# Attention and a GELU network in one kernel: filler matmuls, batch 0's v behind its k, masks as items of their own, late query tiles in the next chunk's layer 1

## The chip, the core and the metric

The kernel runs on one core of a Trainium2 chip. Five engines work side by side, each through its own program in order: TensorE (PE: matrix products from the on-chip memory SBUF into PSUM), VectorE (DVE), ScalarE (ACT: exponential, GELU), GpSimd (POOL) and SyncE (SP). An engine that has to wait for another holds up all that stands behind in its own program. POOL and SP also issue the transfers (DMAs); those from POOL can change the type from 32-bit to 16-bit floats on the way. The metric is the device time of one execution in microseconds; lower is better.

## The reference

Two parts, one after the other. First causal attention over 8 batches and 8 heads, 576 positions of 64 elements, with a decay that a running sum over the positions makes:

```python
scores = scale * np.matmul(q, k.transpose(0, 1, 3, 2))
causal = np.triu(np.ones((S, S), dtype=bool), k=1)
cum = np.cumsum(np.maximum(s, 0.0), axis=-1)
bias = -(cum[:, :, :, None] - cum[:, :, None, :])
scores = np.where(causal, -1000000000.0, scores + np.minimum(bias, 0.0))
scores = scores - np.max(scores, axis=-1, keepdims=True)
attn = np.exp(scores)
attn = attn / (np.sum(attn, axis=-1, keepdims=True) + 1e-09)
attn_out = np.matmul(attn, v)
```

Then, with the eight heads side by side, x has 4608 rows (tokens) of 512, and goes through a network of two layers with 2048 units:

```python
h = x @ w_in
g = 0.5 * h * (1.0 + erf(h * inv_sqrt2))
out = g @ w_out
```

## The kernel before

Matrix products run on 16-bit inputs. The decay makes far keys vanish, so the kernel computes scores for a band of key and query blocks alone, and at its end tests from the data that this was allowed (`cert_1` to `cert_4`); a general path behind a branch is there for other data and isn't taken here.

**Tiling.** The 4608 tokens are cut into nine chunks of 512. A batch has 576 tokens, in five query tiles `it` of 128 (the last of 64). Heads go in two groups `g` of four, and the band's scores of a group come in two units `u`, each of 128 x 512 for each head. So a batch has four score items `sc(b, g, u)` and ten items `av(b, g, it)` that multiply by v. Tiles 0 and 1 need unit 0 alone, tile 2 both units, tiles 3 and 4 unit 1.

**The work of a batch b.** `load_qks(b)` has 16 transfers on POOL's queue (L91) and `load_v(b)` five (L113, SP's queue; POOL's for batch 1). `tr_qk` (L177, VectorE) transposes q and k, `den_col` (L208) and `scale_v` (L200, VectorE) put v with its weights into `vv`, `absmax` (L184, VectorE, 2.5 us each) and `square_v` (L192, ScalarE) gather what the test at the end needs. `sc_item` computes scores (L320, TensorE), their exponentials (L328, ScalarE) into P, and multiplies the blocks on the diagonal by a triangular mask (L332, and L337 for unit 1, VectorE). `av_item` multiplies (L396, TensorE), then VectorE takes the reciprocal of the sums (L405) and scales into `x` (L406). With the second group done, `to_xT` writes the transposed tile into `xT`: by DMA from SP's queue (L375) in batches above 0, by TensorE (L379) and a VectorE copy (L382) in batch 0. In batch 0 `sc_first` takes the place of `sc_item`: the mask is added on TensorE (L362).

**The network on a chunk c.** `l1_item(c, f2)` for f2 = 0 to 7: eight matmuls (L424) into PSUM `h_ps`, then a GELU on ScalarE (L429) into `gT`. It reads all 512 tokens of the chunk in `xT` at once (chunk 0: in halves of 256). `l2_item` then takes the four row blocks (`sub`) of 128 tokens, sixteen matmuls each (L440) into PSUM `o_ps`, a VectorE copy (L447) and a DMA to the output (L449).

**Order.** It is written out by hand. While chunk c is in layer 2, the attention of batch b = c + 1 is woven in: `groups` cuts a row block into four slots of four matmuls and runs side items after each. Preparation of batch b on VectorE (`tr_qk`, `den_col`, `scale_v`, `absmax`) stands between layer 1 and layer 2 of chunk c in the program (L529 to L536); VectorE reaches it early, since little of its program lies in layer 1. Chunk 8 has no attention beside it, and neither has layer 2 of chunk 7. Chunk c reaches into batch c by 512 - 64c tokens: query tiles 0 to 3 of batch 1 for chunk 1, tiles 0 to 2 for chunks 2 and 3, tiles 0 and 1 for chunks 4 and 5, tile 0 for 6 and 7.

**Buffers.** In PSUM, two of tag `sc` (scores and `h_ps`, two banks each), two of `av`, two of `mlp` (`o_ps` and the filler's output). In SBUF, two each of P, raw q/k, raw v, `qkT` and `vv`, six of `x`, one `gT`. So row block n + 2 waits for the copy of row block n, and an av item waits for the scaling of the av item two before.

**The head.** POOL issues q and k of batch 0, then eight weight blocks (`load_w`, L137), then q and k of batch 1, then v of batch 1. At most eight of its transfers are under way: each issue from the ninth on waits for the one eight before it.

The layer 2 of chunks 1 to 6 stands in the program so:

```python
groups(c, (0,), [[], [], [(sc, b, 0, 0)], []])
groups(c, (1,), [[(sc, b, 1, 0)], [], [(sc, b, 0, 1), (av, b, 0, 0)], [(av, b, 0, 1)]])
groups(c, (2,), [[(sc, b, 1, 1), (gelu_set,), (av, b, 1, 0)], [(av, b, 1, 1)], [(av, b, 0, 2)], [(av, b, 0, 3), (av, b, 0, 4)]])
groups(c, (3,), [[(av, b, 1, 2)], [(av, b, 1, 3)], [(av, b, 1, 4)], []])
```

## Time and profile before

| | us |
|---|---|
| median of 3 runs | 350.01 |
| lowest, highest | 348.54, 350.91 |
| the profiled execution, its own time | 350.83 |
| its span in the profile | 349.1 |

| stage | from, to | span |
|---|---|---|
| head | 0 to 31.0 | 31.0 |
| chunk 0, layer 1 | 31.0 to 49.9 | 18.9 |
| chunk 0, layer 2 | 49.9 to 77.2 | 27.3 |
| chunk 1 | 77.2 to 112.0 | 34.8 |
| chunk 2 | 112.0 to 148.3 | 36.3 |
| chunks 3 to 6 | 148.3 to 286.6 | 138.3 |
| chunk 7 | 286.6 to 314.9 | 28.3 |
| chunk 8 and the end | 314.9 to 349.1 | 34.2 |

How to read the lines below. The page gives busy time of each engine, and the chain of work that ended last, followed back from the end. A line of the timeline has start and duration in us, engine, line of the kernel, operation, output and inputs, shape and count; in brackets stands the engine's idle time before it and what ended it. A line of the chain has start, duration and what it was. A row of busy time by stage has the stretch, its length, busy time (and instructions) of PE, PE's weight loads, DVE, ACT and POOL, the clock granted to TensorE, the DMA share and GB/s. Matmuls are pipelined and their ends are modelled, so the time from one start to the next says more than a duration; some matmul records are missing, so a count of 63 can stand for 64.

### The profile page before, as it was taken

The page shows a single profiled execution, that of the slowest core. Times are in us where ns is not written, and L with a number is a line of the kernel's source. Part 1 is how long each engine was busy: PE and PEld are TensorE (multiplying, and loading weights), DVE is VectorE, ACT ScalarE, POOL GpSimd, SP SyncE. Part 2 cuts the span into 40 slices and gives each one's busy share as a digit, 9 for nine tenths or more (in the row PEclk, how much of TensorE's full clock was granted, in tenths as well). Part 3 has the DMA queues.
Part 4 walks back from the last instruction along what each step waited for, and adds up shares of the span by engine and source line. Part 5 has one row for each costly group of instructions (what it writes and reads, how often), then busy time and mean ns, then how long its engine had stood idle before and what let it go on. Part 6 is the DMA issues. An engine that isn't in the chain of part 4 may idle for free.

```text
span 349.1 us, 6207 instructions
## 1 busy us (share of the span) xinstructions
PE 316.1 (91%) x2467; PEld 156.4 (45%) x2508; DVE 187.7 (54%) x392; ACT 182.9 (52%) x243; POOL 88.0 (25%) x149
## 2 busy tenths in 40 slices
PE   0998997779999999799999999999999999999992
PEld 0326863444444444344444444444544444444441
DVE  7233688678458915891479247925792570141020
ACT  2433594728871887067727872777178715304400
POOL 8832598810460082008200640000000000000000
PEclk9999999989999999999999999999999999999998
DMA  8999999989594786478657685700410051020011
GB/s 98 210 206 207 148 190 116 178 154 223 85 140 115 173 82 100 108 173 82 85 107 188 64 105 107 188 2 32 120 39 0 33 121 39 0 90 33 1 61 68
DMA packets 98868, 37.27 MB, mean 107 GB/s; under 512 B 89776, under 2 KB 93872, under 8 KB 98832
## 3 DMA queue, kind: packets, MB, share of 16 engines
q0 software_dynamic: 43504, 14.82, 37.0%
q1 hardware_dynamic: 55328, 21.98, 25.0%
q8 instruction: 21, 0.34, 0.5%
q14 instruction: 15, 0.12, 0.1%
HBM read 36.85 MB, written 9.44 MB: 133 GB/s over the span
## 4 chain that ended last, share of the span: by engine, by line
PE 70%; DMA 12%; POOL 7%; ACT 4%; DVE 3%; issue 2%; POOLq 0%
PE h_ps L424 32%; PE o_ps L440 29%; DMA w_out_r<-in_moe_w_out_dram 6%; POOL raw_qk L91 6%; PE sc_ps L320 5%; PE av L396 4%; ACT P L328 4%; DMA raw_v<-in_v_dram 2%; DMA raw_qk<-in_k_dram 2%; DMA xT<-x 2%; DVE P L332 1%; DMA raw_qk<-in_q_dram 1%; DVE x L406 1%; POOL raw_v L113 1%; POOL w_out_r L137 1%
## 5 line engine op out<-in xcount | busy, mean ns | idle before, releaser
L440 PE MATMUL o_ps<-w_out_r,gT 128*128 128x512 bf16 x545 | 135.7, 382 | 3.7 <-DVE o_sb L447 2.0
L424 PE MATMUL h_ps<-xT,w_in_r 128*128 128x512 bf16 (+1 forms) x632 | 128.9, 361 | 4.9 <-DMA xT<-x 3.5
L429 ACT ACTIVATE gT<-h_ps 128x1024 bf16<-128x1024 f32 (+1 forms) x80 | 75.1, 938 | 103.2 <-PE h_ps L424 99.6
L424 PEld LDWEIGHTS <-w_in_r 128*128 128x128 bf16 x640 | 62.6, 99 | 67.9 <-issue 6.5
L440 PEld LDWEIGHTS <-gT 128*128 128x128 bf16 x576 | 51.2, 98 | 55.5 <-issue 6.1
L328 ACT ACTIVATE P<-sc_ps 128x1024 bf16<-128x1024 f32 x56 | 54.3, 1021 | 25.1 <-PE sc_ps L320 25.1
L91 POOL DMA_DIRECT2D raw_qk<-in_q_dram x64 | 38.8, 627 | 104.4 <-DVE amx L184 94.4
L332 DVE TENSOR_TENSOR P<-P,tri_bf 128x1024 bf16<-128x1024 bf16 x28 | 19.3, 691 | 68.7 <-ACT P L328 68.7
L447 DVE COPY o_sb<-o_ps 128x512 f32<-128x512 f32 x36 | 24.7, 686 | 49.5 <-PE o_ps L440 49.5
L91 POOL DMA_DIRECT2D raw_qk<-in_k_dram x64 | 38.7, 633 | 10.5 <-DMA w_out_r<-in_moe_w_out_dram 7.8
L184 DVE TENSOR_REDUCE amx<-raw_qk 128x2 f32<-128x2304 bf16 x16 | 40.0, 2536 | 0.0
L396 PE MATMUL av<-vv,P 128*128 128x65 bf16 x576 | 31.3, 200 | 8.6 <-DVE x L406 8.6
L396 PEld LDWEIGHTS <-P 128*128 128x128 bf16 x576 | 26.0, 102 | 26.4 <-DVE x L406 18.5
L406 DVE TENSOR_TENSOR x<-av,rc 128x256 bf16<-128x256 f32 (+1 forms) x80 | 33.8, 423 | 2.8
L200 DVE TENSOR_TENSOR vv<-raw_v,wb 128x512 bf16<-128x512 f32 (+1 forms) x40 | 25.6, 692 | 4.0 <-DMA raw_v<-in_v_dram 3.8
L177 DVE STREAM_TRANSPOSE qkT<-raw_qk 128x576 f32<-128x576 f32 x32 | 22.4, 749 | 6.4 <-DMA raw_qk<-in_q_dram 5.5
L192 ACT ACTIVATE sq<-raw_v 128x512 bf16<-128x512 f32 (+1 forms) x40 | 24.9, 623 | 0.0
L405 DVE RECIPROCAL rc<-av 128x4 f32<-128x4 f32 (+1 forms) x80 | 14.0, 175 | 20.0 <-PE av L396 19.9
L320 PE MATMUL sc_ps<-qkT 32*128 32x256 bf16 (+2 forms) x560 | 20.6, 250 | 0.0
L320 PEld LDWEIGHTS <-qkT 32*128 32x128 bf16 x560 | 13.0, 92 | 13.9 <-issue 13.0
L366 ACT ACTIVATE P<-sc_ps 128x1024 bf16<-128x1024 f32 x8 | 8.2, 1023 | 12.2 <-PE sc_ps L362 12.2
L354 PE MATMUL sc_ps<-qkT 32*128 32x256 bf16 (+2 forms) x80 | 10.4, 356 | 2.1 <-DVE qkT L177 1.4
(74 smaller groups left out, 82.8 us busy)
## 6 DMA issues: line engine op xcount, KB each, us to landing
out_dram<-o_sb SPq DMA_DIRECT2D x36, 256.0 KB, 2.2
raw_v<-in_v_dram SPq DMA_DIRECT2D x28, 256.0 KB, 3.9
raw_qk<-in_q_dram POOLq DMA_DIRECT2D x64, 72.0 KB, 2.9
raw_qk<-in_k_dram POOLq DMA_DIRECT2D x64, 72.0 KB, 3.1
w_in_r<-in_moe_w_in_dram POOLq DMA_DIRECT2D x4, 512.0 KB, 11.7
w_out_r<-in_moe_w_out_dram POOLq DMA_DIRECT2D x4, 512.0 KB, 18.2
raw_v<-in_v_dram POOLq DMA_DIRECT2D x4, 256.0 KB, 4.0
raw_v<-in_v_dram SPq DMA_DIRECT2D x7, 128.0 KB, 3.5
```

The source lines that it names most:

```text
L91: nc.gpsimd.dma_start(out=raws[b, "qk"][h * 32 : h * 32 + 32, i, g, :].rearrange("p (t c) -> p t c", c=2 * D), in_=bass.AP(tensor=src.tens ...
L184: nc.vector.tensor_reduce(amx[:, b * HG + g], raws[b, "qk"][:, :, g, :], axis=AX, op=ALU.max, apply_absolute_value=True,)
L192: nc.scalar.activation(sq[:n_st], raws[b, "v"][:n_st, st].rearrange("p h d -> p (h d)"), func=AF.Square, accum_out=sumv[:n_st, b, st : st ...
L200: nc.vector.tensor_tensor(vv[b % 2][:n_st, st, :, 0:D], raws[b, "v"][:n_st, st, :, :], w.unsqueeze(2).to_broadcast([n_st, H, D]), op=MULT,)
L320: nc.tensor.matmul(s_ps[h // 2][:, h % 2, off : off + n], lhsT=qk[r, 1, g, jt * 128 : jt * 128 + 128, e], rhs=qk[r, 0, g, i0 : i0 + n, e], ...
L328: nc.scalar.activation(P[:, 2 * h2 : 2 * h2 + 2, o : o + 512], s_ps[h2], func=AF.Exp, scale=scale)
L396: nc.tensor.matmul(o_ps[:, h, :], lhsT=P[:, h, off : off + 128], rhs=vv[b % 2][:, jt, 4 * g + h, :], start=(i == 0), stop=(i == len(BLK[it ...
L406: nc.vector.tensor_tensor(x_of[b, it][:n, g * 256 : g * 256 + 256].rearrange("p (h d) -> p h d", d=D), o_ps[:n, :, 0:D], rc[:n].unsqueeze( ...
L424: nc.tensor.matmul(h_ps[:, i, n0:n1], lhsT=w_in_r[:, ko, ft * 128 : (ft + 1) * 128], rhs=xT[:, ko, c * NB + n0 : c * NB + n1], start=(ko = ...
L429: nc.scalar.activation(gT_of[c][:, f2 * 2 : f2 * 2 + 2, n0:n1], h_ps[:, :, n0:n1], func=AF.Gelu)
L440: nc.tensor.matmul(y_of[c, sub], lhsT=gT[:, ft, sub * 128 : (sub + 1) * 128], rhs=w_out_r[:, ft, :], start=(ft == 0), stop=(ft == FT - 1),)
L447: nc.vector.tensor_copy(o_sb, y_of[c, sub])
```

## The change

- **Fillers.** `zero` is set first on VectorE, and dummy matmuls on zeros (`filler(n)`, 512 columns each) go into TensorE's program: 16 ahead of `weights()`, 4 behind it, and 6, 4, 4, 1 and 1 between the items of batch 0. The two memsets for `ident` and `uptri` pass from POOL to VectorE.
- **v behind k.** Of batch 0's v, tiles 0 and 1 stay on SP's queue; tiles 2 to 4 go to POOL's, behind batch 0's k and ahead of the weights. Scores of batch 0 fill both banks together, and their order with the v products is new. `masks()` stands later in the program.
- **Chunk 0, layer 2.** `absmax(1)` goes from ahead of layer 2 to behind it. Scores, masks and av items have new slots, `load_v(2)` is issued behind row block 1, query tile 4 of batch 1 goes to layer 1 of chunk 1, and tiles 2 and 3 are transposed by TensorE.
- **Masks apart.** `sc_item` ends with the exponentials; `mk_item` holds the multiplication by the mask, in a slot of its own.
- **Chunks 1 to 6, layer 2.** Score items stand in slots 2, 5, 7, 10 (batches 2 and 3) or 2, 5, 8, 11 of sixteen, masks in 5, 8, 11, 13 (14), av items of tiles 0 and 1 in 6, 7, 9, 10; in batches 2 and 3 tile 2 follows in 12 and 13.
- **Late query tiles.** The other av items of batch c (tile 4 for chunk 1, tiles 3 and 4 for chunks 2 and 3, tiles 2 to 4 from chunk 4 on) are woven into layer 1 of chunk c, one behind each step f2, and with them the preparation of batch c + 1.

```diff
+    zero = const.tile([128, NB], bf16, name="zero")
+    nc.vector.memset(zero, 0.0)
     ident = const.tile([128, 128], fp32, name="ident")
-    make_identity(nc, ident)
+    nc.vector.memset(ident, 0.0)
+    make_identity(nc, ident, nomemset=True)
...
+    def mk_item(b, g, u):
+        P = P_of[b, g]
+        o = UO[u]
         d = P[:, :, o : o + 512].rearrange("p e (g c) -> p e g c", c=256)[:, :, :, 0:128]
         nc.vector.tensor_tensor(
             d, d, tri_bf.unsqueeze(1).unsqueeze(1).to_broadcast([128, 4, 2, 128]), op=MULT
...
     exp_set()
+    filler(16)
     weights()
+    filler(4)
     tr_qk(0, 0, 0)
     v0 = raw_v(0)
-    nc.vector.memset(v0[0:1, :, 0, 0:1], 0.0)
-    load_v(0, nc.sync)
-    masks()
-    tr_qk(0, 1, 0)
+    nc.vector.memset(v0[0:1, 0:2, 0, 0:1], 0.0)
+    load_v(0, nc.sync, range(2))
+    load_v(0, nc.gpsimd, range(2, ST))
     for i in range(4):
         load_w(0, i)
     for i in range(4):
         load_w(1, i)
     load_qks(1)
     load_v(1, nc.gpsimd)
+    masks()
+    tr_qk(0, 1, 0)
     sc_first(0, 0)
+    filler(6)
     sc_first(0, 1)
+    filler(4)
     den_col(0)
     tr_qk(0, 0, 1)
     scale_v(0, 0)
+    tr_qk(0, 1, 1)
     scale_v(0, 1)
-    tr_qk(0, 1, 1)
+    sc_first(1, 0)
     av_item(0, 0, 0)
     av_item(0, 0, 1)
...
+    late_of = {1: [(0, 4), (1, 4)]}
+    for c in range(2, B):
+        late_of[c] = [(g, it) for it in range(3 if c < 4 else 2, ST) for g in range(HG)]
...
             for f2 in range(FT // 2):
                 l1_item(c, f2)
+                for g, it in late_of.get(c, [])[f2 : f2 + 1]:
+                    av(c, g, it)
+                if b < B and f2 < HG:
+                    tr_qk(b, 0, f2)
+                    tr_qk(b, 1, f2)
+                if b < B and f2 == 2:
+                    den_col(b)
+                    for st in range(2):
+                        scale_v(b, st)
+                if b < B and f2 == 3:
+                    for st in range(2, ST):
+                        scale_v(b, st)
+                if b < B and 4 <= f2 < 4 + HG:
+                    absmax(b, f2 - 4)
...
         if b < B:
-            for g in range(HG):
-                for i in range(2):
-                    tr_qk(b, i, g)
-            den_col(b)
-            for st in range(ST):
-                scale_v(b, st)
-            for g in range(HG):
-                absmax(b, g)
+            if c == 0:
+                for g in range(HG):
+                    for i in range(2):
+                        tr_qk(b, i, g)
+                den_col(b)
+                for st in range(ST):
+                    scale_v(b, st)
             exp_set()
             if c == 0:
                 l2_item(c, (0,))
-                groups(c, (1,), [[(sc, b, 0, 0)], [], [(sc, b, 0, 1)], []])
+                groups(c, (1,), [[], [(sc, b, 0, 0)], [], [(sc, b, 0, 1), (mk, b, 0, 0)]])
+                load_v(2, nc.sync)
+                groups(c, (2,), [
+                    [(av, b, 0, 0)],
+                    [(sc, b, 1, 0), (av, b, 0, 1)],
+                    [(mk, b, 0, 1)],
+                    [(sc, b, 1, 1), (av, b, 0, 2), (mk, b, 1, 0)],
+                ])
                 groups(c, (3,), [
+                    [(av, b, 1, 0)],
+                    [(av, b, 1, 1), (mk, b, 1, 1)],
+                    [(av, b, 0, 3), (av, b, 1, 2, True)],
+                    [(av, b, 1, 3, True), (to_xT, b, 2, True), (to_xT, b, 3, True)],
                 ])
...
+                side = [[] for _ in range(16)]
+                sc_at = (2, 5, 7, 10) if b < 4 else (2, 5, 8, 11)
+                for at, (g, u) in zip(sc_at, [(0, 0), (1, 0), (0, 1), (1, 1)]):
+                    side[at].append((sc, b, g, u))
+                side[sc_at[3]].append((gelu_set,))
+                for at, (g, u) in zip((5, 8, 11, 13 if b < 4 else 14), [(0, 0), (1, 0), (0, 1), (1, 1)]):
+                    side[at].append((mk, b, g, u))
+                for at, (g, it) in zip((6, 7, 9, 10), [(0, 0), (0, 1), (1, 0), (1, 1)]):
+                    side[at].append((av, b, g, it))
+                if b < 4:
+                    side[12].append((av, b, 0, 2))
+                    side[13].append((av, b, 1, 2))
+                for sub in range(4):
+                    groups(c, (sub,), side[4 * sub : 4 * sub + 4])
```

More of the change, by code (lines that the diff above doesn't have):

```diff
@@ L15 @@
 from concourse._compat import with_exitstack
-from concourse.masks import make_identity, make_upper_triangular
+from concourse.masks import make_identity
 @with_exitstack
@@ L161 @@
         nc.vector.memset(t[64:128, ST - 1, :, :], 0.0)
-    zero = const.tile([128, NB], bf16, name="zero")
-    nc.vector.memset(zero, 0.0)
     nc.vector.memset(sumv, 0.0)
@@ L308, with scores @@
     P_of, x_of = {}, {}
-    def sc_item(b, g, u):
-        if u == 0:
-            P_of[b, g] = work.tile([128, 4, PW], bf16, tag="P", bufs=2, name="P")
-        P = P_of[b, g]
-        qk = qkT[b % 2]
+    def scores(qk, g, u, masked=False):
         s_ps = [ps.tile([128, 2, 512], fp32, tag="sc", bufs=2, name="sc_ps") for _ in range(2)]
@@ L323, in sc_item @@
                         rhs=qk[r, 0, g, i0 : i0 + n, e],
-                        start=(e == 0), stop=(e == 1), tile_position=(h * 32, 0),
+                        start=(e == 0), stop=(not masked and e == 1), tile_position=(h * 32, 0),
                     )
+            for h in range(4 if masked else 0):
+                m = min(n, 128)
+                nc.tensor.matmul(
+                    s_ps[h // 2][:, h % 2, off : off + m], lhsT=ident_bf, rhs=neg_bf[:, :m],
+                    start=False, stop=True,
+                )
+        return s_ps
+    def sc_item(b, g, u):
+        if u == 0:
+            P_of[b, g] = work.tile([128, 4, PW], bf16, tag="P", bufs=2, name="P")
+        P = P_of[b, g]
+        s_ps = scores(qkT[b % 2], g, u)
         o = UO[u]
@@ L411, in av_item @@
         )
-        if g == HG - 1 and b > 0:
+        if g == HG - 1 and b > 0 and not later:
             to_xT(b, it)
```

83 lines of the change are left out of this document (29 added, 54 removed).

## The prediction

> **What bounds the kernel now.** I read the page first (busy shares, the chain that ended last), then busy time by stage, then the timeline where a stage holds idle TensorE.
>
> ```profile
> PE 316.1 (91%) x2467; PEld 156.4 (45%) x2508; DVE 187.7 (54%) x392; ACT 182.9 (52%) x243; POOL 88.0 (25%) x149
> PE 70%; DMA 12%; POOL 7%; ACT 4%; DVE 3%; issue 2%; POOLq 0%
> ```
>
> TensorE is 91% busy and 70% of the chain. Nothing here takes real TensorE work away, so a gain can only be idle or slow TensorE time. The stages, cut where layer 1 of a chunk starts (span, TensorE busy, VectorE busy in columns 2, 3 and 5):
>
> ```profile
> 49.90:77.20 27.30, 21.10 (x214) 10.85 (x216) 19.17 (x43) 14.72 (x23) 18.32 (x31) 0.94 1.17 151
> 77.20:112.00 34.80, 33.38 (x275) 15.94 (x281) 22.62 (x50) 21.55 (x28) 9.52 (x16) 1.00 0.80 145
> 112.00:148.30 36.30, 33.38 (x275) 15.90 (x280) 23.40 (x45) 21.55 (x28) 9.57 (x16) 1.00 0.69 116
> 148.30:286.60 138.30, 132.83 (x1100) 64.02 (x1121) 86.03 (x166) 86.19 (x112) 19.15 (x32) 1.00 0.48 90
> 286.60:314.90 28.30, 28.14 (x131) 12.68 (x132) 5.56 (x27) 8.18 (x8) 0.00 (x0) 1.00 0.16 45
> ```
>
> The first row is layer 2 of chunk 0, with 6.2 us idle. Then come chunk 1 (34.8), chunk 2 (36.3), chunks 3 to 6 (138.3, or 34.57 each) and chunk 7 (28.3), whose layer 2 has no attention beside it.
>
> **The head (fillers, v behind k).** Layer 1 of chunk 0, and the last key transpose ahead of it:
>
> ```profile
> 17.26 0.78 DVE L177 STREAM_TRANSPOSE qkT<-raw_qk 128x576 f32<-128x576 f32 x1 [0.58 <-DMA raw_qk<-in_k_dram]
> ...
> 31.00 1.87 PE L424 MATMUL h_ps<-xT,w_in_r 128*128 128x256 bf16 x8 [0.73 <-DVE xT L382]
> ...
> 35.27 1.11 PE L424 MATMUL h_ps<-xT,w_in_r 128*128 128x256 bf16 x8
> ```
>
> The same eight matmuls take 1.87 us at 31.0 and 1.11 at 35.3, so TensorE ran at half rate until about 35 us, whatever the clock column says. Fillers keep it busy from about 1 us, and should have it at full rate when the first scores come. After the key transpose (18.0) there remain two score items, four exponentials of 1.0 us (1.94 for two, below), the attention-times-v items and two transposes, some 7 us: layer 1 starts near 25 in place of 31. It lasts 18.9 us now (31.0 to 49.9) and loses about 2 us to the half rate, so layer 2 of chunk 0 starts near 42: a lead of 0 (no warming) to 9, I take 8. It is worth less than that, because of the next wait.
>
> **Layer 2 of chunk 0.** POOL's queue, the chain, and VectorE with TensorE:
>
> ```profile
> 36.90 0.60 POOL L91 DMA_DIRECT2D raw_qk<-in_k_dram  x1 [1.94 <-DMA w_out_r<-in_moe_w_out_dram]
> 39.45 0.60 POOL L91 DMA_DIRECT2D raw_qk<-in_k_dram  x1 [1.95 <-DMA w_out_r<-in_moe_w_out_dram]
> ...
> 44.78 4.26 POOL L113 DMA_DIRECT2D raw_v<-in_v_dram  x5
> ```
> ```profile
> 47.45 6.26 DMA raw_v<-in_v_dram
> ```
> ```profile
> 53.73 1.29 DVE L200 TENSOR_TENSOR vv<-raw_v,wb 128x512 bf16<-128x512 f32 x2 [2.41 <-DMA raw_v<-in_v_dram]
> ...
> 54.94 5.00 DVE L184 TENSOR_REDUCE amx<-raw_qk 128x2 f32<-128x2304 bf16 x2
> ...
> 59.86 0.67 DVE L447 COPY o_sb<-o_ps 128x512 f32<-128x512 f32 x1
> ...
> 60.59 1.02 PE L440 MATMUL o_ps<-w_out_r,gT 128*128 128x512 bf16 x4 [1.98 <-DVE o_sb L447]
> ```
>
> POOL issues one q/k load of batch 1 each time a weight block lands (every 2.55 us), the rest after the last one at 39.2, then v: batch 1's v lands at 53.7. The program still puts scale_v of batch 1 ahead of the copy of row block 0 on VectorE, and row block 2 needs that copy's PSUM buffer. Only the 5.0 us of absmax leave this place. So the copy comes at 55.0 and row block 2 can start at 55.7, not 60.59: 4.9 us won. With the full lead TensorE has done row blocks 0 and 1 by 50 and idles 5.9 us; with none it gets there at 58.6, and 2.0 are won. A lead above 3 us buys nothing.
>
> The three v loads of batch 0 that pass from SP's queue to POOL's, ahead of the weights, cost 0.9 us of issue each (4.26 for five). POOL's queue holds transfers then, so the weights land at the same rate and the bytes are the same; I bound their landing at 0.4 earlier (two memsets leave POOL) to 0.9 later (less v beside the q/k issue), and take 0, the nearest to the steady 2.55. POOL serves nothing else that waits.
>
> The gap has its own price:
>
> ```profile
> 69.86 1.90 PE L440 MATMUL o_ps<-w_out_r,gT 128*128 128x512 bf16 x4
> ...
> 77.24 2.97 PE L424 MATMUL h_ps<-xT,w_in_r 128*128 128x512 bf16 x13 [1.92 <-DMA xT<-x]
> ```
>
> Four matmuls took 1.90 us at 69.86, 1.02 at 60.59. After 2 us of idle (58.6 to 60.59) the rate held; after sparse work it was half. Dense work from 31.0 took 4.2 us to win it back, so I charge half of that, 2.1 us (0 to 4). The Trainium skill ("TensorE: Matmul & The Clock Gate", Part 1 and "HAM oscillation") speaks against the change here: an idle window of about 3.4 us halves the clock, and a busy one restores it. By that page the price would be half of 3.4 to 6.8, 1.7 to 3.4 us, and the sum 0.5 lower to 1.2 higher; the 69.86 row agrees that the rate falls, no row shows a clean 5.9 us gap.
>
> From row block 2 to layer 1 of chunk 1 it takes 16.65 us now (60.59 to 77.24). New: 32 matmuls at 0.216 (6.9), two score items (1.4), 56 av matmuls at 0.03 (1.7), half rate (2.1), waits for masks moved behind (0.9 + 0.8, worked out under chunks 1 and 2), and the last chain of av, reciprocal, scaling, TensorE transpose and two copies in place of the DMA transpose (2.4): 16.2. Layer 1 of chunk 1 starts at 71.9, not 77.24: **5.3 us won** (bounds 3 to 7.5). Absmax, cert_decay and 5 us of VectorE now lie in layer 1 of chunk 1, under 14 us of TensorE.
>
> **Chunks 3 to 6.** The layer 2 from 231.31 to 252.06, TensorE, then VectorE, then ScalarE:
>
> ```profile
> 231.31 2.75 PE L440 MATMUL o_ps<-w_out_r,gT 128*128 128x512 bf16 x11
> ...
> 236.39 0.89 PE L320 MATMUL sc_ps<-qkT 32*128 32x256 bf16 x16
> ...
> 243.34 0.30 PE L396 MATMUL av<-vv,P 128*128 128x65 bf16 x4 [0.73 <-DVE x L406]
> ...
> 246.12 0.41 PE L396 MATMUL av<-vv,P 128*128 128x65 bf16 x8 [0.36 <-DVE x L406]
> ...
> 249.85 0.41 PE L396 MATMUL av<-vv,P 128*128 128x65 bf16 x8
> 250.10 1.02 PE L440 MATMUL o_ps<-w_out_r,gT 128*128 128x512 bf16 x4
> ...
> 252.06 2.11 PE L424 MATMUL h_ps<-xT,w_in_r 128*128 128x512 bf16 x9
> ```
> ```profile
> 241.84 0.69 DVE L332 TENSOR_TENSOR P<-P,tri_bf 128x1024 bf16<-128x1024 bf16 x1 [1.95 <-ACT P L328]
> ...
> 242.65 0.17 DVE L405 RECIPROCAL rc<-av 128x4 f32<-128x4 f32 x1
> ...
> 250.29 0.18 DVE L405 RECIPROCAL rc<-av 128x4 f32<-128x4 f32 x1 [0.47 <-PE av L396]
> 250.51 0.42 DVE L406 TENSOR_TENSOR x<-av,rc 128x256 bf16<-128x256 f32 x1
> ...
> 252.26 0.69 DVE L447 COPY o_sb<-o_ps 128x512 f32<-128x512 f32 x1 [0.24 <-PE o_ps L440]
> ```
> ```profile
> 234.66 1.94 ACT L328 ACTIVATE P<-sc_ps 128x1024 bf16<-128x1024 f32 x2 [0.83 <-PE sc_ps L320]
> ```
>
> The 20.75 us are 64 matmuls (13.82), four score items (3.17), 72 av matmuls (eight in 0.25: 2.2) and 1.56 of waits. The waits come from VectorE's order: the mask at 241.84 stands idle 1.95 us for its exponentials, and the reciprocal behind it, whose av was ready, frees an av buffer only at 243. With the mask as an item of its own, placed three slots after its scores, reciprocals come first and the waits go. The score item at 236.39 waits for the exponentials that end at 236.60; three slots apart instead of two it doesn't: 0.25. Six av items (48 matmuls, 1.44 us) move to layer 1 of the next chunk. New: layer 2 13.82+2.9+0.75 = 17.5; layer 1 13.82+1.44 = 15.3; 32.75 a chunk, 32.3 in chunk 3 with four late items. Sum 130.55 against 138.3: **7.75 won** (bounds 3 to 9). Chunk 7 takes six late items without giving any: **1.45 lost**.
>
> What hides the moved items is VectorE's room in layer 1:
>
> ```profile
> 218.30 2.75 DVE L177 STREAM_TRANSPOSE qkT<-raw_qk 128x576 f32<-128x576 f32 x4
> ...
> 221.04 3.13 DVE L200 TENSOR_TENSOR vv<-raw_v,wb 128x512 bf16<-128x512 f32 x5
> 224.10 5.00 DVE L184 TENSOR_REDUCE amx<-raw_qk 128x2 f32<-128x2304 bf16 x2
> ```
>
> That is 10.9 us, plus six reciprocals and scalings at 0.6 and a copy at 0.7: 15.2 of 15.3 us. Worked through in order, the av item at step 5 finds its PSUM buffer free 2.6 us ahead, and the queue ends about 2 us into layer 2, where the first copy is due 4 us in.
>
> **Chunks 1 and 2.** Here the next chunk needs query tile 2, so it stays in slots 12 and 13, behind masks in slots 11 and 13. The mask in 11 stands behind the copy of row block 2: 0.2 + 0.69 + 0.81 (241.84 to 242.65), less one slot of 0.86: 0.9 us of wait. The mask in 13 stands behind the scaling of the item before: 1.08 (249.85 to 250.93) + 0.81, less 1.1: 0.8. Then the transposed tile goes by DMA:
>
> ```profile
> xT<-x SPq DMA_TRANSPOSE x35, 2.4
> ```
> ```profile
> 144.38 3.72 DMA xT<-x
> ```
>
> It lands 2.4 to 3.7 after 1.1 of VectorE, with 2.0 of TensorE work left: 1.6 to 2.9, I take 2.2. Layer 2: 13.82 + 2.9 + 1.2 (40 av matmuls) + 0.1 + 0.9 + 0.8 + 2.2 = 21.9; with layer 1 at 14.3 and 14.8, 36.2 and 36.7 against 34.8 and 36.3: **1.8 lost** (bounds -2 to 4).
>
> **Sum.** -5.3 - 7.75 + 1.45 + 1.8 = -9.8. Span 349.1 becomes 339.3; the profiled run's own 350.83 becomes 341.0. The median of the runs, 350.01, is 0.8 below that run, so 340.2.
>
> **Rivals.** (a) The lead isn't eaten. If batch 1's v came before 50, layer 2 would run through: 42 + 8.7 + 14 = 64.7, 12.5 won instead of 5.3: 333. Against it: after 39.45 POOL still issues 9.6 us. (b) TensorE stays at half rate through row blocks 2 and 3, since each mask wait breaks the dense work: 10 us of work doubled, less the 2.1 counted and 3 of waits that vanish: 345.1. The 69.86 row speaks for it. The Trainium skill (same page, "A second HAM failure mode") describes such micro-idling; 69.47 to 73 agrees. (c) The mask change doesn't do what it says: the av items wait for exponentials, not for VectorE's order, and chunks 3 to 6 stay at 34.57: 348. Against it, exponentials end at 236.60 and the next av is slots later. (d) The other side: VectorE in layer 1 becomes the bound. Beyond 2.6 us of lateness every us stops TensorE for one in each of chunks 3 to 6; 5.9 us late costs 3.3 each, 13.2 in all, and ends at 353.5, later still slower. Against it, VectorE idles long stretches of layer 2 today.
>
> **How the numbers follow.** Forecast 0.61, (a) 0.06, (b) 0.15, (c) 0.12, (d) 0.06. Faster by over 1% means under 346.5, about what a measurement can tell from none: the forecast nearly whole, (a), most of (b), a fifth of (c): 0.79. Slower is (d), 0.06; the rest 0.15. The range 335.5 to 347 takes in the bounds of the terms and (b), and leaves out (a), (d) and part of (c).
>
> **What would show it.** Layer 1 of chunk 0 near 25 with 256-column matmuls at 0.11 us; row block 2 starting near 55.7 after a wait on the copy, and four matmuls in about 1.9 us behind it; chunk 1 from 72; chunks 4 to 6 at 32.75 with no av wait in layer 2; a DMA wait for xT of some 2 us after chunks 1 and 2. Wrong: row block 2 before 53, chunks 4 to 6 above 34, or av waits in layer 1.

## The result, and the profile after

| | before | changed | ratio, 95% interval |
|---|---|---|---|
| median, us | 350.46 | 339.45 | 0.9693, 0.9616 to 0.977 |
| lowest, highest | 348.54, 350.91 | 336.93, 341.56 | |
| span of the profiled execution | 349.1 | 339.8 | |

Four runs of each on one chip: the changed kernel is 3.1% faster. Its profiled execution (341.56) is the longest of its four, so the spans (9.3 apart) show a little less than the medians (11.0).

The page of the changed kernel, busy shares and the chain that ended last:

```profile
PE 312.7 (92%) x2546; PEld 156.3 (46%) x2546; DVE 192.0 (57%) x396; ACT 182.3 (54%) x243; POOL 90.4 (27%) x150
...
PE 76%; DMA 9%; POOL 7%; DVE 4%; issue 1%; POOLq 0%
```

TensorE's share of the chain rose from 70% to 76%. Busy time by stage, again cut where layer 1 of a chunk starts (stretch, span, TensorE, its weight loads, VectorE, ScalarE, POOL, granted clock, DMA share, GB/s):

```profile
40.40:71.30 30.90, 21.73 (x210) 10.46 (x208) 18.59 (x47) 14.72 (x23) 19.16 (x30) 0.89 1.11 176
71.30:107.90 36.60, 32.66 (x264) 15.63 (x265) 26.56 (x45) 21.55 (x28) 19.12 (x32) 0.99 1.07 143
107.90:146.30 38.40, 36.02 (x280) 16.89 (x280) 22.36 (x42) 21.55 (x28) 9.57 (x16) 0.92 0.61 101
146.30:275.90 129.60, 129.60 (x1105) 63.59 (x1106) 87.17 (x163) 86.19 (x112) 19.14 (x32) 1.00 0.50 96
275.90:305.60 29.70, 29.70 (x183) 14.12 (x182) 9.20 (x38) 8.18 (x8) 0.00 (x0) 1.00 0.15 47
```

In chunks 3 to 6 TensorE is busy in all of 129.60 us: no idle time is left to win there. Behind the head, what is idle lies in layer 2 of chunk 0 (9.2 us) and in chunks 1 and 2 (3.9 and 2.4). The timeline of the changed kernel shows where (start, duration, engine, line, operation, shape, count, idle time before and what ended it):

```profile
23.22 1.03 PE L425 MATMUL h_ps<-xT,w_in_r 128*128 128x256 bf16 x8 [0.61 <-DVE xT L383]
...
54.91 1.87 PE L441 MATMUL o_ps<-w_out_r,gT 128*128 128x512 bf16 x4 [5.92 <-DVE o_sb L448]
...
59.70 1.89 PE L441 MATMUL o_ps<-w_out_r,gT 128*128 128x512 bf16 x8
...
71.34 1.89 PE L425 MATMUL h_ps<-xT,w_in_r 128*128 128x512 bf16 x8 [1.75 <-DVE drop L255]
...
73.30 1.89 PE L425 MATMUL h_ps<-xT,w_in_r 128*128 128x512 bf16 x8
...
101.09 0.39 PE L397 MATMUL av<-vv,P 128*128 128x65 bf16 x7 [0.49 <-DVE P L350]
...
102.81 0.39 PE L397 MATMUL av<-vv,P 128*128 128x65 bf16 x7 [0.44 <-DVE P L350]
...
107.94 3.57 PE L425 MATMUL h_ps<-xT,w_in_r 128*128 128x512 bf16 x8 [3.02 <-DMA xT<-x]
111.31 0.65 PE L397 MATMUL av<-vv,P 128*128 128x65 bf16 x8
111.77 2.90 PE L425 MATMUL h_ps<-xT,w_in_r 128*128 128x512 bf16 x8
...
114.75 1.89 PE L425 MATMUL h_ps<-xT,w_in_r 128*128 128x512 bf16 x8
...
146.30 1.89 PE L425 MATMUL h_ps<-xT,w_in_r 128*128 128x512 bf16 x8 [1.41 <-DMA xT<-x]
```

Layer 1 of chunk 0 starts at 23.22 at full rate (eight in 1.03). TensorE then waits 5.92 us for the copy, runs the next eight at half rate, and has its rate back at 59.70 (eight in 1.89). At 107.94 it has waited 3.02 us for a DMA transpose, and again runs at half rate. The VectorE work that the 5.92 us wait stands on:

```profile
52.98 1.29 DVE L205 TENSOR_TENSOR vv<-raw_v,wb 128x512 bf16<-128x512 f32 x2 [0.92 <-DMA raw_v<-in_v_dram]
54.19 1.27 DVE L448 COPY o_sb<-o_ps 128x512 f32<-128x512 f32 x2
```

Where the time went, from the starts of layer 1 in the two timelines:

| stage | before | changed | difference | predicted |
|---|---|---|---|---|
| up to layer 1 of chunk 1 | 77.24 | 71.34 | -5.90 | -5.3 |
| chunk 1 | 34.77 | 36.60 | +1.83 | +1.4 |
| chunk 2 | 36.33 | 38.36 | +2.03 | +0.4 |
| chunks 3 to 6 | 138.30 | 129.56 | -8.74 | -7.75 |
| chunk 7 | 28.27 | 29.71 | +1.44 | +1.45 |
| span | 349.1 | 339.8 | -9.3 | -9.8 |

These are two single executions. The lengths of chunks 4 to 6 repeat to 0.02 us wherever their code is the same; the start of layer 1 of chunk 1 doesn't. e3 below leaves chunk 0 as in the kernel before and has it at 74.31 in place of 77.24; e5 and e6 leave it as in the changed kernel and have it at 71.85 and 71.04 for 71.34. So the 5.90 of the first row is 2.5 to 6.2 by which of these executions are paired.

### The profile page after: what moved, and what is told of

Its sections match the earlier page's. It is cut to its first block, busy times and chain, and to the rows that moved or that the text cites. A ratio compares the mean times of both kernels' runs of the same rounds, so it can differ in the third digit from the quotient of the medians.

```text
span 339.8 us, 6336 instructions
## 1 busy us (share of the span) xinstructions
PE 312.7 (92%) x2546; PEld 156.3 (46%) x2546; DVE 192.0 (57%) x396; ACT 182.3 (54%) x243; POOL 90.4 (27%) x150
## 4 chain that ended last, share of the span: by engine, by line
PE 76%; DMA 9%; POOL 7%; DVE 4%; issue 1%; POOLq 0%
PE h_ps L425 33%; PE o_ps L441 33%; DMA w_out_r<-in_moe_w_out_dram 6%; PE av L397 5%; PE sc_ps L321 4%; POOL raw_qk L91 4%; DMA xT<-x 2%; POOL raw_v L113 1%; DMA raw_v<-in_v_dram 1%; DVE P L350 1%; DVE o_sb L448 1%; DVE x L407 1%; POOL w_in_r L137 1%; POOL w_out_r L137 1%; DVE vv L205 0%
## 5 line engine op out<-in xcount | busy, mean ns | idle before, releaser
L425 PE MATMUL h_ps<-xT,w_in_r 128*128 128x512 bf16 (+1 forms) x640 | 136.0, 363 | 7.0 <-DMA xT<-x 4.4
L425 PEld LDWEIGHTS <-w_in_r 128*128 128x128 bf16 x640 | 60.1, 98 | 63.5 <-issue 11.7
L441 PEld LDWEIGHTS <-gT 128*128 128x128 bf16 x576 | 52.5, 98 | 64.1 <-issue 9.8
L397 PEld LDWEIGHTS <-P 128*128 128x128 bf16 x576 | 27.7, 98 | 20.8 <-DVE P L350 4.7
L182 DVE STREAM_TRANSPOSE qkT<-raw_qk 128x576 f32<-128x576 f32 x32 | 23.3, 758 | 12.9 <-DMA raw_qk<-in_q_dram 9.0
L321 PE MATMUL sc_ps<-qkT 32*128 32x256 bf16 (+2 forms) x640 | 22.7, 253 | 2.2 <-DVE qkT L182 1.7
L389 PE MATMUL f_ps<-zero 128*128 128x512 bf16 x36 | 10.6, 435 | 1.2 <-DVE zero L140 1.2
```

What stands on the lines that cost most here:

```text
L321: nc.tensor.matmul(s_ps[h // 2][:, h % 2, off : off + n], lhsT=qk[r, 1, g, jt * 128 : jt * 128 + 128, e], rhs=qk[r, 0, g, i0 : i0 + n, e], ...
L397: nc.tensor.matmul(o_ps[:, h, :], lhsT=P[:, h, off : off + 128], rhs=vv[b % 2][:, jt, 4 * g + h, :], start=(i == 0), stop=(i == len(BLK[it ...
L425: nc.tensor.matmul(h_ps[:, i, n0:n1], lhsT=w_in_r[:, ko, ft * 128 : (ft + 1) * 128], rhs=xT[:, ko, c * NB + n0 : c * NB + n1], start=(ko = ...
L441: nc.tensor.matmul(y_of[c, sub], lhsT=gT[:, ft, sub * 128 : (sub + 1) * 128], rhs=w_out_r[:, ft, :], start=(ft == 0), stop=(ft == FT - 1),)
```

## The experiments

Nothing is left out of the computation in any of them. Each ratio is to the kernel before, timed on the same chip (its median there was 349.4 for e1, e2, e3 and e10, 349.12 for e4 to e7, 350.23 for the rest). L1(1) is the start of layer 1 of chunk 1; the columns behind it are the lengths of chunks 1, 2, 3 and of each of 4 to 6, all from the profiled execution.

| run | median, us | ratio, 95% interval | L1(1) | 1 | 2 | 3 | 4 to 6 |
|---|---|---|---|---|---|---|---|
| before | 350.46 | | 77.24 | 34.77 | 36.33 | 34.57 | 34.58 |
| changed | 339.45 | 0.9693, 0.9616 to 0.977 | 71.34 | 36.60 | 38.36 | 32.02 | 32.51 |
| e1 no fillers | 338.66 | 0.9678, 0.9614 to 0.9742 | 70.12 | 37.36 | 35.50 | 32.03 | 32.51 |
| e2 masks in | 343.6 | 0.9804, 0.9743 to 0.9864 | 72.06 | 38.20 | 37.06 | 33.97 | 32.56 |
| e3 before, masks apart | 343.72 | 0.9849, 0.9784 to 0.9915 | 74.31 | 34.09 | 34.95 | 33.89 | 33.89 |
| e10 before, absmax behind | 345.0 | 0.985, 0.9787 to 0.9913 | 72.29 | 36.42 | 36.26 | 34.57 | 34.57 |
| e14 late tiles alone | 347.91 | 0.994, 0.9907 to 0.9972 | 70.62 | 38.24 | 37.17 | 35.06 | 33.88 |
| e4 scale_v behind | 339.39 | 0.9711, 0.9647 to 0.9775 | 71.61 | 37.71 | 35.48 | 32.02 | 32.52 |
| e7 v of batch 2 later | 338.4 | 0.9682, 0.9612 to 0.9753 | 69.96 | 36.58 | 37.09 | 32.03 | 32.51 |
| e5 tile 2 by TensorE | 334.27 | 0.9561, 0.9495 to 0.9627 | 71.85 | 33.66 | 34.14 | 32.03 | 32.51 |
| e6 and masks earlier | 331.69 | 0.9493, 0.9426 to 0.956 | 71.04 | 32.70 | 32.86 | 32.03 | 32.51 |
| e8 = e4, e6, e7 | 326.1 | 0.9315, 0.9272 to 0.9358 | 65.87 | 32.38 | 32.86 | 32.03 | 32.51 |
| e11 all tiles by TensorE | 325.55 | 0.9293, 0.9265 to 0.9321 | 66.52 | 32.38 | 32.86 | 32.03 | 32.51 |
| e12 = e11, no fillers | 329.98 | 0.9422, 0.9387 to 0.9457 | 67.77 | 33.17 | 32.86 | 32.17 | 32.51 |

e1, e2, e3 and e10 ran on one chip, e4 to e7 on a second, e8, e11, e12 and e14 on a third.

### The lead of the head

**e1: the changed kernel without its fillers.**

```diff
     exp_set()
-    filler(16)
     weights()
-    filler(4)
...
     sc_first(0, 0)
-    filler(6)
     sc_first(0, 1)
-    filler(4)
...
```

> The changed kernel without any of its 36 filler matmuls. My theory (a lead in the head above some 3 us buys nothing, because row block 2 of chunk 0 waits for a copy that stands behind batch 1's v): layer 1 of chunk 0 starts later than 23.2 us and runs partly at half rate, layer 2 starts 4 to 7 us after 40.4, and row block 2 still starts within 2 us of 54.9; the whole time is within 3 us of the changed kernel's 339.5. Rival (the fillers carry the gain of chunk 0): row block 2 starts 4 us or more later, near 59, and the time is 343 or more.

Its timeline:

```profile
45.72 5.34 PE L441 MATMUL o_ps<-w_out_r,gT 128*128 128x512 bf16 x24
...
54.22 1.04 PE L441 MATMUL o_ps<-w_out_r,gT 128*128 128x512 bf16 x4
...
70.12 3.57 PE L425 MATMUL h_ps<-xT,w_in_r 128*128 128x512 bf16 x8 [3.07 <-DMA xT<-x]
```

Layer 2 of chunk 0 starts 5.3 us later than with fillers (45.72 against 40.44), finds its copies done, and runs through at full rate: row block 2 starts at 54.22 for 54.91, with no gap and no half rate in front of it. Layer 1 of chunk 1 starts 1.2 us earlier than with fillers. The medians (338.66 and 339.45) can't be told apart. The lead that the fillers win is all lost at the copy, as forecast.

**e10: the kernel before, with `absmax(1)` alone moved behind layer 2 of chunk 0.**

```diff
-            for g in range(HG):
+            for g in range(HG if c > 0 else 0):
                 absmax(b, g)
             exp_set()
...
                 load_v(2, nc.sync)
+                for g in range(HG):
+                    absmax(b, g)
```

> The kernel before, with absmax of batch 1 alone moved behind layer 2 of chunk 0. Theory: the copy of row block 0 comes at 55.0 instead of 59.9, TensorE no longer waits for it, row block 2 starts at 58.6 instead of 60.6, and layer 1 of chunk 1 some 2 us earlier (75); the whole time is 348. Rival (the wait is for batch 1's v, so nothing is won): row block 2 stays at 60 or later.

```profile
55.79 1.90 PE L440 MATMUL o_ps<-w_out_r,gT 128*128 128x512 bf16 x8
...
72.29 8.05 PE L424 MATMUL h_ps<-xT,w_in_r 128*128 128x512 bf16 x29 [2.25 <-DMA xT<-x]
```

In its timeline row block 2 follows row block 1 without a wait, and layer 1 of chunk 1 starts at 72.29, 5.0 earlier than before, where some 2 were expected; of that 1.65 goes back in chunk 1, whose first matmuls run at half rate. By medians on one chip it is 1.5% faster (345.0 against 349.4), from one moved call, without the head's lead. How much of the 5.0 is the moved call's stays open. Layer 2 of chunk 0 starts 1.8 earlier here (48.15 for 49.93), ahead of the call. And e3, which has `absmax(1)` in its old place, takes 24.5 us from that start to layer 1 of chunk 1, where e10 takes 24.1 and the kernel before 27.3. In e3's execution `absmax(1)` could start earlier (52.67 for 54.94), the copy behind it came in time, and row block 2 had no wait either:

```profile
52.67 5.00 DVE L184 TENSOR_REDUCE amx<-raw_qk 128x2 f32<-128x2304 bf16 x2
57.59 0.67 DVE L453 COPY o_sb<-o_ps 128x512 f32<-128x512 f32 x1
```

### Chunks 3 to 6: which of three edits did it

**e2: the changed kernel, the mask back at the end of the score item.**

```diff
                 P[:, 2 * h2 : 2 * h2 + 2, o : o + 512], s_ps[h2], func=AF.Exp, scale=scale
             )
+        mk_now(b, g, u)

     def mk_item(b, g, u):
+        pass
+
+    def mk_now(b, g, u):
```

> The changed kernel with each mask straight behind its exponentials again, all else as changed. Theory of the prediction (masks apart take the av waits out of layer 2): the 1.56 us of waits come back and chunks 4 to 6 take about 34.0 us in place of 32.5; the whole time rises by some 6 us. Rival (score items three slots apart, and six av items fewer in layer 2, suffice): VectorE is held up by the masks as before, but two PSUM buffers cover it, and chunks 4 to 6 stay within 0.4 us of 32.5.

**e3: the kernel before, with masks as items of their own in chunks 1 to 6.**

```diff
...
-                groups(c, (1,), [[(sc, b, 1, 0)], [], [(sc, b, 0, 1), (av, b, 0, 0)], [(av, b, 0, 1)]])
+                groups(c, (1,), [
+                    [(sc, b, 1, 0)], [(mk, b, 0, 0)], [(sc, b, 0, 1), (av, b, 0, 0)],
+                    [(mk, b, 1, 0), (av, b, 0, 1)],
+                ])
...
-                    [(av, b, 1, 1)],
+                    [(mk, b, 0, 1), (av, b, 1, 1)],
                     [(av, b, 0, 2)],
-                    [(av, b, 0, 3), (av, b, 0, 4)],
+                    [(mk, b, 1, 1), (av, b, 0, 3), (av, b, 0, 4)],
```

> The kernel before, with the masks of chunks 1 to 6 alone as items of their own (slots 5, 7, 9 and 11; scores and av items where they were). Theory of the prediction: most of the 1.56 us of av waits in each layer 2 go, and chunks 4 to 6 take about 33.2 us in place of 34.57; the whole time is about 342 to 344. Rival (spacing and late tiles are what counts): chunks 4 to 6 stay above 34.2, the time within 2 us of 350.

**e14: late query tiles alone from chunk 3 on.** Masks as in e2, and the slots of scores and av items that the kernel before has.

```diff
-                sc_at = (2, 5, 7, 10) if b < 4 else (2, 5, 8, 11)
+                sc_at = (2, 5, 7, 10) if b < 4 else (2, 4, 6, 8)
...
-                for at, (g, it) in zip((6, 7, 9, 10), [(0, 0), (0, 1), (1, 0), (1, 1)]):
+                for at, (g, it) in zip((6, 7, 9, 10) if b < 4 else (6, 7, 8, 9), [(0, 0), (0, 1), (1, 0), (1, 1)]):
```

> The changed kernel with masks straight behind the exponentials, and in batches 4 to 8 scores and av items in the slots that they had before (2, 4, 6, 8 and 6, 7, 8, 9), so that of the change only the late query tiles act in chunks 3 to 6. The two waits of av items that now lie in layer 1 (0.52 and 0.16 us) are gone in any case. If the late tiles alone carry the gain of these chunks, the others go too, because two av items fewer wait for a PSUM buffer: within 0.3 us of 32.5. If the spacing of the scores is needed, the 0.73 and 0.15 of waits for PSUM buffers and the 0.25 of the score item stay: 33.4 to 33.7 in chunks 4 to 6.

The prediction gave the masks the credit. The timelines of e2 (VectorE, then TensorE), e3 and e14 in chunk 5 or 6:

```profile
270.31 0.69 DVE L354 TENSOR_TENSOR P<-P,tri_bf 128x1024 bf16<-128x1024 bf16 x1 [1.97 <-ACT P L342]
270.92 0.18 DVE L410 RECIPROCAL rc<-av 128x4 f32<-128x4 f32 x1
```
```profile
272.74 0.29 PE L401 MATMUL av<-vv,P 128*128 128x65 bf16 x4
```
```profile
241.69 0.42 PE L402 MATMUL av<-vv,P 128*128 128x65 bf16 x8 [0.79 <-DVE x L412]
```
```profile
242.27 0.30 PE L401 MATMUL av<-vv,P 128*128 128x65 bf16 x4 [0.73 <-DVE x L411]
```

In e2 the mask still stands 1.97 us idle for its exponentials, with the reciprocal behind it, just as in the kernel before. But the av item that needs the freed buffer comes only at 272.74, a score item and two groups of matmuls later, and doesn't wait: chunks 5 and 6 take 32.51, as with masks apart. So e2's rival came out, to the hundredth. In e3 and e14 one wait of 0.7 to 0.8 us is left, and neither length is one that was expected: e3's 33.89 lies between 33.2 and 34.2, e14's 33.88 above both 32.5 and 33.4 to 33.7. From the lengths of chunks 4 to 6:

| what is changed | length | won |
|---|---|---|
| masks apart (e3) | 33.89 | 0.69 |
| late tiles (e14) | 33.88 | 0.70 |
| late tiles and spacing (e2, chunks 5 and 6) | 32.51 | 2.07 |
| all three (changed) | 32.51 | 2.07 |

So with late tiles in place the spacing (of scores and av items) is worth 1.37 us a chunk, and masks apart nothing more. No run has spacing without late tiles, so whether spacing alone would do is open. In chunks 1 to 3 e2 is 2.25 us longer than the changed kernel (109.23 against 106.98), mostly where a wait passes into half rate. At the end of chunk 2 it has this:

```profile
147.32 3.36 PE L429 MATMUL h_ps<-xT,w_in_r 128*128 128x512 bf16 x8 [2.20 <-DMA xT<-x]
```

The changed kernel waits 1.41 us there and keeps its rate; the 2.20 us and the half rate behind them make chunk 3 33.97 in place of 32.02. By spans e2 is 3.0 us longer than the changed kernel; the intervals of the two ratios just overlap. The rise that the theory expected (some 6 us) came in part, but out of chunks 1 to 3 and not out of 4 to 6.

### Chunks 1 and 2: the transpose by DMA

**e5: tile 2 of batches 2 and 3 transposed by TensorE and copied by VectorE**, as the change does it in chunk 0.

```diff
-                    side[13].append((av, b, 1, 2))
+                    side[13].append((av, b, 1, 2, True))
+                    side[14].append((to_xT, b, 2, True))
```

> The changed kernel with query tile 2 of batches 2 and 3 transposed by TensorE in slot 14 in place of the DMA. Theory: the waits for xT ahead of chunks 2 and 3 (3.0 and about 1.4 us) go, and with the first the half rate that follows it (3.57 and 2.71 us for eight matmuls, against 1.73): chunk 1 takes 33.5 to 34, chunk 2 about 34; the whole time is 332 to 334. Rival (the half rate has another cause, or the copy becomes the wait): the DMA wait turns into a wait on the copy of 1 us or more, and the first matmuls of chunk 2 stay slow; 337 or more.

**e6: e5, and the last two masks of these batches in slots 10 and 11.**

```diff
-                for at, (g, u) in zip((5, 8, 11, 13 if b < 4 else 14), [(0, 0), (1, 0), (0, 1), (1, 1)]):
+                for at, (g, u) in zip((5, 8, 10, 11) if b < 4 else (5, 8, 11, 14), [(0, 0), (1, 0), (0, 1), (1, 1)]):
```

> As the one with tile 2 transposed by TensorE, and in batches 2 and 3 the masks of unit 1 two slots earlier (10 and 11), ahead of the copy of row block 2 and of the scaling of tile 2's first item. Theory: the two av waits of each of these layers 2 (0.68 and 0.63 us from one start to the next at 100.41 and 102.18) go too: 1.3 us less in each of chunks 1 and 2 than with the transposes alone, 2.5 us in all. Rival (the exponentials, not VectorE's order, bind the masks): the waits stay, no difference above 0.5 us.

The timeline of e5, then of e6:

```profile
104.42 0.39 PE L380 MATMUL xt_ps<-ident_bf,x 128*128 128x128 bf16 x4
...
105.51 1.89 PE L425 MATMUL h_ps<-xT,w_in_r 128*128 128x512 bf16 x8
```
```profile
100.12 0.41 PE L397 MATMUL av<-vv,P 128*128 128x65 bf16 x8
...
103.74 1.89 PE L425 MATMUL h_ps<-xT,w_in_r 128*128 128x512 bf16 x8 [0.16 <-DMA xT<-x]
```

In e5 layer 1 of chunk 2 starts without a wait and at full rate, and chunks 1 and 2 fall by 7.16 together (74.96 to 67.80): about the waits of 3.02 and 1.41 and 2.9 of half rate (below), less eight small matmuls. e6 takes the mask waits too (none before the av row at 100.12), another 2.24. By ratios the two are worth 4.6 us (0.9693 to 0.9561, on two chips, the intervals overlapping a little) and 2.4 (0.9561 to 0.9493; on one chip, with all four runs of e6 below all four of e5). The ratio gives e5 less than the lengths do, in part because the changed kernel's profiled execution is the longest of its four.

### Chunk 0: copy, v and SP's queue

**e4: the scalings of v behind row block 1.** The copy no longer waits for batch 1's v.

```diff
                 den_col(b)
-                for st in range(ST):
-                    scale_v(b, st)
             exp_set()
...
                 groups(c, (1,), [[], [(sc, b, 0, 0)], [], [(sc, b, 0, 1), (mk, b, 0, 0)]])
+                scale_v(b, 0)
+                scale_v(b, 1)
...
-                    [(mk, b, 0, 1)],
+                    [(mk, b, 0, 1), (scale_v, b, 3)],
```

> The changed kernel with scale_v of batch 1 moved behind the copies of row blocks 0 and 1 on VectorE, woven between the items of row blocks 2 and 3. Theory (row block 2 waits for v of batch 1 only because of VectorE's order): row block 2 starts near 50 in place of 54.9, the gap of 5.9 us goes, its matmuls run at full rate (four in 1.02 us), and layer 1 of chunk 1 starts at 65 to 68 in place of 71.3; the whole time is 333 to 336. Rival (v's landing is needed anyway, or the clock isn't the gap's doing): the wait moves to the av items, layer 1 of chunk 1 starts at 70 or later.

**e7: the v loads of batch 2 issued behind layer 2 of chunk 0**, not behind its row block 1.

```diff
-                load_v(2, nc.sync)
                 groups(c, (2,), [
...
                 load_qks(2)
+                load_v(2, nc.sync)
```

> The changed kernel with load_v of batch 2 issued behind row block 3 of chunk 0, as before the change, instead of behind row block 1. Theory (the 1.75 us that layer 1 of chunk 1 waits, which the profile puts down to a VectorE instruction, are the DMA transposes of tiles 0 and 1, which stand behind load_v(2) on SP's queue until 67.45 though their inputs are ready from 64.9): they start at 64.9 and 66, and layer 1 of chunk 1 at 70.1 in place of 71.34. Rival (the wait is VectorE's, as named): 71.3 stays.

The timeline of e4 on TensorE, then on SP's queue:

```profile
49.96 1.02 PE L441 MATMUL o_ps<-w_out_r,gT 128*128 128x512 bf16 x3 [0.83 <-DVE o_sb L448]
...
71.61 0.59 PE L425 MATMUL h_ps<-xT,w_in_r 128*128 128x512 bf16 x1 [7.54 <-DMA xT<-x]
```
```profile
51.12 10.87 SPq L113 DMA_DIRECT2D raw_v<-in_v_dram  x5
62.04 1.43 SPq L450 DMA_DIRECT2D out_dram<-o_sb  x1
63.57 2.88 SPq L376 DMA_TRANSPOSE xT<-x  x2
```

The gap is gone (0.83 for 5.92), row block 2 starts 5.0 us earlier at full rate, and yet layer 1 of chunk 1 starts no earlier: 7.54 us of wait stand there, and the 65 to 68 that were expected did not come. The rival's late start came, but for neither of its reasons. SP was busy from 51.12 to 61.99 with issuing v of batch 2, five loads in 10.87 us, and the DMA transposes of tiles 0 and 1 could only go at 63.57. The changed kernel and e7 on the same queue, and e7 on TensorE:

```profile
56.08 10.60 SPq L113 DMA_DIRECT2D raw_v<-in_v_dram  x5
...
67.45 2.63 SPq L376 DMA_TRANSPOSE xT<-x  x2
```
```profile
64.73 2.61 SPq L376 DMA_TRANSPOSE xT<-x  x2
...
69.06 2.96 SPq L113 DMA_DIRECT2D raw_v<-in_v_dram  x4
```
```profile
69.96 1.89 PE L425 MATMUL h_ps<-xT,w_in_r 128*128 128x512 bf16 x7 [0.52 <-DVE xT L383]
```

With v later (four loads then take 2.96 us to issue) the transposes go 2.7 us earlier, and layer 1 of chunk 1 starts 1.4 earlier (69.96, where the three executions with `load_v(2)` ahead, the changed kernel, e5 and e6, have 71.04 to 71.85), now behind a copy. The medians can't tell e7 from the changed kernel (ratios 0.9682 and 0.9693). So the changed kernel's wait of 1.75 at 71.34, which the trace puts down to a VectorE instruction of line 255, was the transposes'.

**e8: e4, e6 and e7 together.**

```diff
-                for st in range(ST):
-                    scale_v(b, st)
...
-                load_v(2, nc.sync)
...
                 load_qks(2)
+                load_v(2, nc.sync)
...
+                    side[14].append((to_xT, b, 2, True))
```

> Three edits together on the changed kernel: scale_v of batch 1 behind the copies, load_v of batch 2 behind row block 3, and in batches 2 and 3 tile 2 by TensorE with its masks earlier. With scale_v alone the xT copy ended at 64.5 but layer 1 of chunk 1 waited until 71.6 for the DMA transposes, which stood behind load_v(2) on SP's queue until 63.6. Theory: without load_v(2) ahead they start at 59.3 and 60.5 and layer 1 of chunk 1 starts at 64.6 to 66.5; then 32.7, 32.9, 32.0, three times 32.5, 29.7 and 34.3 follow: a span near 325, a time of 325 to 329. Rival (the transposes are late because the transfers of batches 1 and 2 fill the DMA engines until about 64, whatever stands on SP's queue): layer 1 of chunk 1 starts at 69 or later, the time is 330 or more.

**e11: e8, and tiles 0 and 1 of batch 1 by TensorE too**, so that no DMA transpose is left in chunk 0.

```diff
-                    [(av, b, 1, 0), (scale_v, b, 4)],
-                    [(av, b, 1, 1), (mk, b, 1, 1)],
-                    [(av, b, 0, 3), (av, b, 1, 2, True)],
-                    [(av, b, 1, 3, True), (to_xT, b, 2, True), (to_xT, b, 3, True)],
+                    [(av, b, 1, 0, True), (scale_v, b, 4)],
+                    [(av, b, 1, 1, True), (mk, b, 1, 1)],
+                    [(to_xT, b, 0, True), (av, b, 0, 3), (av, b, 1, 2, True)],
+                    [(av, b, 1, 3, True)] + [(to_xT, b, it, True) for it in (1, 2, 3)],
```

> As the one with the three edits, and tiles 0 and 1 of batch 1 also transposed by TensorE, so that no DMA transpose is left ahead of chunk 1. By both theories layer 1 of chunk 1 then starts at 65 to 66, behind the copies on VectorE, and the time is 324 to 327. If the DMA engines were the bind with the three edits, this is 3 us or more faster than that one; if SP's queue was, it is within 1 us of it.

**e12: e11 without fillers** (the edit of e1).

```diff
-    filler(16)
     weights()
-    filler(4)
```

> The kernel with all tiles of batch 1 by TensorE, without any filler. Theory (the fillers' lead buys nothing as long as row block 2 waits for v, and pays once that wait is gone): layer 2 of chunk 0 starts at 45.7 in place of 40.5, the q/k of batch 1 no longer holds it up, row block 2 starts at 54 in place of 50, and layer 1 of chunk 1 3 to 5 us later: the fillers are worth 3 to 5 us here. Rival (the transfers of batch 1 set the end of chunk 0 in any case): within 1.5 us.

TensorE in e8, then in e11, VectorE in e11, TensorE in e12:

```profile
50.40 1.02 PE L441 MATMUL o_ps<-w_out_r,gT 128*128 128x512 bf16 x3 [1.43 <-DVE o_sb L448]
...
65.87 1.89 PE L425 MATMUL h_ps<-xT,w_in_r 128*128 128x512 bf16 x7 [1.36 <-DMA xT<-x]
```
```profile
51.03 1.02 PE L441 MATMUL o_ps<-w_out_r,gT 128*128 128x512 bf16 x3 [1.83 <-DVE o_sb L448]
...
66.52 1.89 PE L425 MATMUL h_ps<-xT,w_in_r 128*128 128x512 bf16 x7 [0.53 <-DVE xT L383]
```
```profile
49.46 0.78 DVE L182 STREAM_TRANSPOSE qkT<-raw_qk 128x576 f32<-128x576 f32 x1 [1.54 <-DMA raw_qk<-in_k_dram]
```
```profile
67.77 1.46 PE L425 MATMUL h_ps<-xT,w_in_r 128*128 128x512 bf16 x5 [0.53 <-DVE xT L383]
```

e4 alone moved layer 1 of chunk 1 by +0.3, e7 alone by -1.4, both by -5.5: each hid the other. In chunk 0 the DMA transposes themselves cost little once no loads stand ahead of them on SP: e8 and e11 can't be told apart by medians. e11 at 325.55 beats both kernels: 7.1% below the one before, where the change has 3.1%. The copy in its chunk 0, for which TensorE still waits 1.83 us, now stands behind batch 1's k: the last transpose waits 1.54 us for it.

Fillers in e11 win 1.25 us up to layer 1 of chunk 1, 2.1 over the span, and 4.4 by medians (325.55 against 329.98, the intervals apart). The medians differ by more than the spans because e11's profiled execution (327.05) is the longest of its seven, 1.5 above their median, and e12's (329.1) is 0.9 below its own. In the medians the 3 to 5 us expected of the fillers are there; the start of layer 1 of chunk 1 moved by 1.25 alone, within the rival's 1.5. In the changed kernel they won nothing.

## Why the prediction came out

The time was forecast as 340.2 and came as 339.45, the span as 339.3 and came as 339.8. That the sum is this near is partly luck: against the forecast the stages up to layer 1 of chunk 1 came out 0.6 us better and chunks 3 to 6 1.0 better, and chunks 1 and 2 2.1 worse. By its steps:

- **Head and the copy: right.** Layer 1 of chunk 0 "near 25" came at 23.22, layer 2 "near 42" at 40.44, row block 2 at 54.91 for 55.7, behind a wait of 5.92 for 5.9. "A lead above 3 us buys nothing" is what e1 shows. Rival (a), a lead that isn't eaten, did not occur; e8, which takes v out of the copy's way, has layer 1 of chunk 1 at 65.87, near the 64.7 that rival (a) gave.
- **From row block 2 to layer 1 of chunk 1: the sum right, two terms wrong.** 16.2 were forecast, 16.43 came. The mask waits were 0.47 and 0.20 of idle for 1.7, and the last chain, put at 2.4, ended in a wait for transposes that SP's queue held up by 1.4 (e7). The two errors offset each other in large part.
- **The price of the gap: right.** 2.1 were charged. Between 54.91 and 59.70 stand eight matmuls of layer 2, four av matmuls at 0.03, a score item and eight av matmuls. Those come to 1.73 + 0.12 + 0.56 + 0.25 = 2.7 at full rate and took 4.8: 2.1 lost. The rate came back in under 5 us, so rival (b), half rate through row blocks 2 and 3, did not occur. (A price of 1.7 to 3.4 in place of 2.1 would move the sum by -0.4 to +1.3, not by the -0.5 to +1.2 that the prediction has.)
- **Chunks 1 and 2: mis-sized, 3.9 lost for 1.8.** The xT wait of 2.2 was right as a mean (3.02 and 1.41), the mask waits were 0.93 of idle for 1.7 in each of the two chunks (1.27 by the starts from 100.41 to 101.32 and from 102.18 to 103.04). The step that failed is what follows a wait: "After 2 us of idle the rate held" rests on the two waits of 2.0 and 1.9 us in the kernel before, and no half rate was charged behind an xT wait that was put at 1.6 to 2.9. From 107.94 to 114.75 TensorE did what takes 3.9 us at full rate (two steps of 1.96, as from 71.34 to 73.30): 2.9 lost, more than the 2.1 by which the sum missed. e5 removes both waits and the half rate.
- **Chunks 3 to 6: the amount right, the cause wrong.** 32.51 for 32.75. "With the mask as an item of its own, placed three slots after its scores, reciprocals come first and the waits go" is the sentence that failed: e2 has masks in and the same 32.51, e3 has masks apart and keeps a wait. The spacing, priced at 0.25, is worth 1.37 on top of late tiles. A part of rival (c) is true then, that the mask edit isn't what does it. That the waits came from VectorE's order still fits (in e3 and e14 the wait left is one for a scaling on VectorE, and e2's masks hold VectorE up as before without stopping TensorE): the spacing gives that order slack.
- **Rival (d), VectorE in layer 1: did not occur.** TensorE is busy in all 129.60 us of chunks 3 to 6.
- **SP's queue: a step that wasn't priced.** `load_v(2)` moved ahead of the DMA transposes, and the prediction followed POOL's queue alone. It costs about 1.4 us in the changed kernel (e7, by one execution), and 5.7 where the copy comes early (71.61 in e4, 65.87 in e8).

## What to carry to other kernels

A moved transfer has to be followed on the queue that issues it: five loads held SP for 10.6 us, and the transposes behind them set when the next layer began. Single edits can mislead both ways, so run the pair before judging either: masks apart won 0.69 us a chunk alone and nothing on top of the other two edits, and two edits that moved a start by +0.3 and -1.4 alone moved it by -5.5 together. Where the last step before dense work is a small tile that arrives by DMA, a transpose by TensorE and a copy took a wait of 1.4 to 3.0 us, and the half rate behind it, off the path.
